# Talking-heads attention with two MLPs: v's matmuls share the slots of the scores' matmuls, first mixings are issued in twos, and GpSimd makes every third high part

## The chip, the cores and the metric

One core of a Trainium2 chip runs the whole program. The metric is device time in microseconds, the median of several runs.

## The reference

A talking-heads attention over 4 batches, 12 heads, 448 tokens and head size 64, and behind it two MLPs. Heads are mixed before and after the softmax:

```python
scores = scale * np.matmul(q, k.transpose(0, 1, 3, 2))
scores = np.einsum('bhij,hg->bgij', scores, w_pre)      # first mixing
scores = scores - np.max(scores, axis=-1, keepdims=True)
attn = np.exp(scores)
attn = attn / (np.sum(attn, axis=-1, keepdims=True) + 1e-09)
attn = np.einsum('bhij,hg->bgij', attn, w_post)         # second mixing
return np.matmul(attn, v).astype(np.float32)
```

The result, as 1792 tokens of width 768, goes through `((x @ w1) * (x @ w2)) @ w3 @ w_out` and then `relu(x @ w_in) ** 2 @ w_out`. Precision near float32 is kept by splitting a number into a high part in a short format and a low part that holds the rest; a product is then three matmuls (high times high, high times low, low times high).

## The kernel before, in words

**Blocks.** A batch's 448 rows are cut into four groups of 110, 110, 110 and 118 rows ("supers", `SUP`), 16 in all; a group is cut into blocks of 10 rows (and one of 8). There are 180 blocks (`BLK`). A block holds 10 rows of all 12 heads, 120 rows for the partitions, so that one matmul with a 120 by 120 matrix mixes the heads.

**The work of one block.** `regroup` (L259) copies the block's scores from the tile `S`, where a row is a partition, into `Bt`, by a DMA of SP's queue. `premix` (L266) is the first mixing, one float32 matmul into a bank of the PSUM ring `ps_p` (three banks). `negmax` (L278) reduces it to the maximum on VectorE; `expo` (L287) takes the exponential on ScalarE with a running sum. `norm` (L301) makes the inverse sums for two blocks at once on VectorE. `split_h` (L317) makes the high part `EH` of exponential times inverse, on VectorE; `split_l` (L325) scales the exponential in place on GpSimd (L328) and subtracts the high part from it, which gives `EL` (L331). `postmix` (L334) is the second mixing, 12 matmuls of float16 into `ps_o` (two banks). `at_h` (L352, ScalarE) and `at_l` (L361, VectorE) bring the result to SBUF as high and low part.

**The work of a group.** `qk` (L215) makes the scores of two heads, six matmuls into the one tile of `ps_s` (two banks), and `evict_s` (L238) copies them to `S` on ScalarE. `av` (L435) multiplies with v: for each pair of heads 24 matmuls in two parts of 12, collected over three pairs in the one bank of `ps_a`; `put_xh` and `put_xl` (L462, L476) read that bank and `store_x` (L484) sends it to memory. `split_q`, `split_ql`, `split_k` and `split_kl` (L197 to L213, L177 to L188) make high parts on VectorE and low parts on GpSimd. `sum_v`, `scale_v`, `split_v` and `split_vl` (L378 to L433) find v's scale and split v; two steps of `scale_v` use TensorE and a bank of `ps_p`.

**The order.** It is written by hand: a loop over slots `u` (L893 to L939) issues, in each slot, `at_h(u-5)`, `premix(u+1)`, `negmax(u)`, `expo(u)`, in even slots `norm(u-2)`, then `split_h(u-2)`, `split_l(u-2)`, `postmix(u-4)`, `at_l(u-5)`, and `regroup(u+4)` last. Work of a group is entered by `at(slot, kind, ...)` into a table of events (L504 to L556); `do(kind)` issues the events of the slot at five places: LOAD ahead of everything, FIRST in front of the exponential, MID and LOW behind `at_l`, END behind those. `qk` and `av` are END events. Every engine works through its own instructions in this order and waits where an operand is not there. From slot 168 on, weights of the MLP are loaded beside the attention, and from slot 170 on decoded; the MLPs follow.

The loop's slots of v's matmuls are offsets from five slots behind the start of the next group:

```python
AV_AT = (0, 1, 1, 2, 3, 3, 5, 6, 6, 7, 8, 8)
slot = first[s + 1] + LAG + 1 + AV_AT[2 * p + part]
at(slot, END, av, s, p, part)
```

Of the kernel before, what the change touches and what calls it, by code (L numbers as in the profile page):

```python
# [24 lines left out]
LEAD = 4  # L25
# [10 lines left out]
def talking_heads_attention_moe_moe2(  # L36
# [222 lines left out]
    def regroup(u):  # L259
        s, m, n = BLK[u]  # L260
        t = bp.tile([NBK, S], F32, tag="Bt", name="Bt", bufs=LEAD + 1)
# [16 lines left out]
    def negmax(u):  # L278

        n, j = BLK[u][2] * H, u % 2  # L280
        if j == 0:
            nsum[u] = nsum[u + 1] = bp.tile([NBK, 4, 2], F32, tag="st", name="st", bufs=3)
# [18 lines left out]
    def norm(u):  # L301

        t = nsum[u]
        rows = [BLK[x][2] * H for x in (u, u + 1)]
        for a in [slice(0, 2)] if rows[0] == rows[1] else [slice(0, 1), slice(1, 2)]:
            n = rows[a.start]
            nc.vector.tensor_scalar(  # L307
                t[:n, 2, a], t[:n, 1, a], 1e-9, 2.0 ** -11, op0=ALU.add, op1=ALU.mult
            )
        for a in [slice(0, 2)] if rows[0] == rows[1] else [slice(0, 1), slice(1, 2)]:  # L310
            n = rows[a.start]
            nc.vector.reciprocal(t[:n, 3, a], t[:n, 2, a])

    def inverse(u):
        return nsum[u][: BLK[u][2] * H, 3, u % 2 : u % 2 + 1]

    def split_h(u):  # L317
        n = BLK[u][2] * H
        hh = bp.tile([NBK, S], F16, tag="EH", name="EH", bufs=4)
        nc.vector.tensor_scalar(  # L320
            hh[:n].rearrange("p (a b) -> p a b", a=EG), Ex[u][:n], inverse(u), None, op0=ALU.mult
        )
        EH[u] = hh

    def split_l(u):  # L325
        n = BLK[u][2] * H
        e = Ex.pop(u)[:n]
        nc.gpsimd.tensor_scalar(e, e, inverse(u), 1.0, op0=ALU.mult, op1=ALU.mult)  # L328
        ll = bp.tile([NBK, S], F16, tag="EL", name="EL", bufs=4)
        a, b = (x[:n].rearrange("p (a b) -> p a b", a=EG) for x in (ll, EH[u]))  # L330
        nc.gpsimd.tensor_tensor(a, e, b, op=ALU.subtract)  # L331
# [60 lines left out]
    def scale_v(b, i):  # L392
# [5 lines left out]
        elif i == 1:  # L398
            vps[b] = pt = psum(ps_p, "p")
# [4 lines left out]
        elif i == 3:  # L404
            vps[b] = pt = psum(ps_p, "p")
# [124 lines left out]
    for b in range(B):  # L530
        f = first[4 * b]
        for hg in range(2):
            at(f - 4 + hg, LOAD, load_v, b, hg)
            for i in range(3):
                at(f + 3 * hg + i + 1, MID, sum_v, b, hg, i)
                at(f + 3 * hg + i + 11, MID, split_v, b, hg, i)
                at(f + 3 * hg + i + 12, LOW, split_vl, b, hg, i)
        for i, kind in enumerate((MID, END, MID, END, MID)):
            at(f + 6 + i, kind, scale_v, b, i)
    AV_AT = (0, 1, 1, 2, 3, 3, 5, 6, 6, 7, 8, 8)  # L540
    for s in range(NSUP - 1):
        for p in range(NDC):
            for part in range(2):
                slot = first[s + 1] + LAG + 1 + AV_AT[2 * p + part]
# [343 lines left out]
    premix(0)  # L888
    mlp_start = first[NSUP - 1]
# [3 lines left out]
    for u in range(NB + LAG + 2):  # L893
# [22 lines left out]
        if u + 1 < NB:  # L916
            premix(u + 1)
# [421 lines left out]
```

## Time and profile before

| | us |
|---|---|
| median of 3 runs | 1352.63 |
| lowest and highest run | 1351.04, 1352.71 |
| the profiled execution | 1354.19 |
| its span, first to last instruction | 1352.5 |
| TensorE busy in the span | 1289.3 (95%) |
| VectorE busy | 1035.0 (77%) |
| ScalarE busy | 712.8 (53%) |
| GpSimd busy | 442.9 (33%) |
| attention: start of the first and last first mixing | 22.3, 468.9 |

The profile is of one execution. Engines are PE (TensorE; PEld is its weight load), DVE (VectorE), ACT (ScalarE), POOL (GpSimd) and SP (a DMA queue). A name such as `EH<-E,st` stands for the tiles written and read, `o` for the bank of the second mixing, `p` for that of the first, `s` for the scores' and `a` for v's. A busy engine is not an engine that sets the time: the chain of waits goes back from the last instruction to what released it, step by step, and shows what does. The shares above are of the whole span; the attention, about a third of it, is read by its own stretches.

### The profile page before, as it was taken

Reading aid. Unit: us, or ns where it says so; the run is one execution under the profiler, and the core shown is the slowest. Engines: PE = TensorE matmul, PEld = TensorE weight load, DVE = VectorE, ACT = ScalarE, POOL = GpSimd, SP = SyncE. Lnnn points to the kernel's source line nnn. Section 1 sums busy time; section 2 is a strip of 40 time slices with the busy share of each in tenths; the row PEclk is TensorE's granted clock in tenths of the full one; section 3 lists DMA queues with packets and bytes.
Section 4 is the critical chain, followed back from the end, with each engine's and each line's share of the span. In section 5 each row is a group of like instructions: output and inputs, shape, how many; then the busy total and the mean of one; then the engine's idle time right before and its main releaser. Section 6 shows DMA issues by size and latency. Waiting matters only on the chain.

```text
span 1352.5 us, 26245 instructions
## 1 busy us (share of the span) xinstructions
PE 1289.3 (95%) x10170; PEld 790.7 (58%) x10170; DVE 1035.0 (77%) x2101; ACT 712.8 (53%) x1365; POOL 442.9 (33%) x511
## 2 busy tenths in 40 slices
PE   5999999999999789999998879999999999999998
PEld 2566666666666554555557855555555555555555
DVE  5999999899899857678836555544667797797866
ACT  3876877876776534444424444435774534535430
POOL 3889789779877621000001200000000000000000
PEclk7999999999999789999999989999999999999999
DMA  5356455544644914344503313400532214223104
GB/s 175 94 140 178 112 143 151 137 121 129 157 112 109 275 53 100 97 110 113 120 17 125 110 47 77 77 6 4 112 71 43 75 48 98 74 36 84 26 13 163
DMA packets 76096, 132.94 MB, mean 98 GB/s; under 512 B 30116, under 2 KB 59940, under 8 KB 75972
## 3 DMA queue, kind: packets, MB, share of 16 engines
q1 hardware_dynamic: 69556, 121.87, 33.7%
q0 software_dynamic: 2992, 5.42, 3.1%
q10 hardware_dynamic: 3424, 3.98, 1.1%
q8 instruction: 80, 1.31, 0.5%
q14 instruction: 44, 0.36, 0.1%
HBM read 80.78 MB, written 11.92 MB: 69 GB/s over the span
## 4 chain that ended last, share of the span: by engine, by line
PE 70%; DVE 19%; DMA 4%; ACT 4%; issue 3%; POOL 1%; SPq 0%; ACTq 0%; POOLq 0%; DVEq 0%
PE mm L982 38%; PE mm L1216 16%; PE p L269 5%; PE o L343 4%; DVE EH L320 3%; DVE ATl L365 3%; DVE st L283 3%; DMA Bt<-S 3%; PE s L229 2%; PE a L452 2%; DVE st L307 1%; DVE Vl L431 1%; PE mm L1088 1%; DVE zt L632 1%; DVE xa L635 1%
## 5 line engine op out<-in xcount | busy, mean ns | idle before, releaser
L982 PE MATMUL mm<-x,w 128*128 128x448 f16 x2304 | 438.9, 353 | 3.3 <-DVE w L717 1.7
L982 PEld LDWEIGHTS <-w 128*128 128x128 f16 x2304 | 225.5, 98 | 215.0 <-issue 2.7
L1216 PE MATMUL mm<-w,g 128*128 128x384 f16 x1344 | 219.7, 326 | 0.0
L269 PE MATMUL p<-Bt,wpre_k 120*120 120x448 f32 x360 | 184.1, 594 | 17.7 <-DMA Bt<-S 16.1
L331 POOL TENSOR_TENSOR EL<-E,EH 120x448 f16<-120x448 f32 x180 | 188.5, 1047 | 15.0
L343 PEld LDWEIGHTS <-EH 120*112 120x112 f16 (+1 forms) x1440 | 133.2, 131 | 90.0 <-issue 89.6
L1216 PEld LDWEIGHTS <-g 128*128 128x128 f16 x1344 | 131.5, 98 | 87.4 <-issue 0.2
L328 POOL TENSOR_SCALAR E<-E,st 120x448 f32<-120x448 f32 x180 | 134.5, 747 | 80.7 <-DVE EH L320 45.6
L291 ACT ACTIVATE E<-p,st 120x448 f32<-120x448 f32 x180 | 115.3, 640 | 57.5 <-DVE st L283 51.6
L343 PE MATMUL o<-wph,EH 120*112 120x120 f16 x720 | 125.7, 218 | 8.6 <-DVE ATl L365 8.4
L359 ACT CAST ATh<-o 112x480 f16<-112x480 f32 x180 | 101.0, 561 | 57.0 <-PE o L343 56.0
L343 PE MATMUL o<-wph,EL 120*112 120x120 f16 x720 | 125.6, 218 | 0.8 <-POOL EL L331 0.8
L343 PE MATMUL o<-wpl,EH 120*112 120x120 f16 x720 | 125.6, 218 | 0.0
L283 DVE TENSOR_REDUCE st<-p 120x1 f32<-120x448 f32 x180 | 110.8, 615 | 17.0 <-PE p L269 16.7
L320 DVE TENSOR_SCALAR EH<-E,st 120x448 f16<-120x448 f32 x180 | 121.3, 674 | 3.1
L1225 DVE SCALAR_TENSOR_TENSOR acc<-mm,sv,acc 128x384 f32<-128x384 f32 x196 | 112.3, 612 | 14.2 <-PE mm L1216 13.5
L653 POOL DMA_DIRECT2D across<-tot x23 | 12.8, 555 | 326.8 <-ACT xa L639 326.8
L639 ACT ACTIVATE xa<-xa 128x768 f32<-128x768 f32 (+1 forms) x72 | 57.2, 795 | 117.3 <-DVE xa L635 107.5
L365 DVE TENSOR_TENSOR ATl<-o,ATh 112x480 f16<-112x480 f32 x180 | 116.3, 646 | 2.7 <-ACT ATh L359 2.3
L982 PE MATMUL mm<-h,M 128*128 128x448 f16 x576 | 110.6, 355 | 1.7 <-ACT M L1010 1.7
L240 ACT COPY S<-s 110x896 f32<-110x896 f32 (+1 forms) x92 | 83.7, 910 | 22.3 <-PE s L229 21.9
L343 PEld LDWEIGHTS <-EL 120*112 120x112 f16 x720 | 94.7, 132 | 0.9 <-POOL EL L331 0.9
(176 smaller groups left out, 1956.5 us busy)
## 6 DMA issues: line engine op xcount, KB each, us to landing
Bt<-S SPq DMA_DIRECT2D x176, 210.0 KB
raw<-in_moe_w_out_dram SPq DMA_DIRECT2D x24, 768.0 KB
raw<-in_moe_w_in_dram SPq DMA_DIRECT2D x16, 768.0 KB
raw<-in_moe_w_dram SPq DMA_DIRECT2D x14, 768.0 KB
raw<-in_moe_w_dram SPq DMA_DIRECT2D x16, 512.0 KB
kraw<-in_k_dram SPq DMA_DIRECT2D x12, 448.0 KB
vraw<-in_v_dram SPq DMA_DIRECT2D x8, 672.0 KB
out_dram<-acc SPq DMA_DIRECT2D x28, 192.0 KB
```

Of the source, the lines that this page charges most:

```text
L269: nc.tensor.matmul(pt[: n * H, :S], wpre_k.rearrange("p t g -> p (t g)")[: n * H, : n * H], Bt.pop(u)[: n * H], start=True, stop=True,)
L283: nc.vector.tensor_reduce(nsum[u][:n, 0, j : j + 1], Pp[u][:n, :S], axis=AX.X, op=ALU.max, negate=True)
L291: nc.scalar.activation(e[:n], Pp.pop(u)[:n, :S].rearrange("p (a b) -> p a b", a=EG), AF.Exp, bias=t[:n, 0, j : j + 1], scale=1.0, accum_ou ...
L320: nc.vector.tensor_scalar(hh[:n].rearrange("p (a b) -> p a b", a=EG), Ex[u][:n], inverse(u), None, op0=ALU.mult)
L328: nc.gpsimd.tensor_scalar(e, e, inverse(u), 1.0, op0=ALU.mult, op1=ALU.mult)
L331: nc.gpsimd.tensor_tensor(a, e, b, op=ALU.subtract)
L343: nc.tensor.matmul(pt[:CP, c * n : (c + 1) * n], a[:n, c * CP : (c + 1) * CP], w[:n, :n], start=(i == 0), stop=(i == 2),)
L359: nc.scalar.copy(ATs[s][0][:, :, :, m * NR : m * NR + nr], src)
L365: nc.vector.tensor_tensor(ATs[s][1][:, :, :, a], src, ATs[s][0][:, :, :, a], op=ALU.subtract)
L982: nc.tensor.matmul(pt[:, :S], w[a][:, cs], x[z][:, sl], start=(c == 0 and i == 0), stop=(c == len(parts) - 1 and i == 2),)
L1216: nc.tensor.matmul(pt[:, :OH], gs[j][a][:, ts_], ws[j][0][:, w, os_], start=(n == 0), stop=(n == 5),)
L1225: nc.vector.scalar_tensor_tensor(d, pt[:, :OH], sv[:, v : v + 1], d, op0=ALU.mult, op1=ALU.add)
```

## The change

Five edits, all in the attention:

1. `regroup` is issued five slots ahead (LEAD 4 to 5), with as many tiles `Bt` as before (five).
2. `norm` writes the sum plus 1e-9, times a constant, three times into `t[:, 2:5, :]`, reading the two columns with a stride of nought; the inverses move to row 5. Only pairs of blocks of unequal size are done one by one.
3. The high part of every block with `u % 3 == 2` is made on GpSimd in `split_l`. The scaled exponential goes to a tile of its own, `F` (one buffer), and not over `E`.
4. Two steps of `scale_v` use the scores' tile `ps_s`, not a bank of `ps_p`; the steps and `split_v`, `split_vl` move one to two slots back.
5. Both parts of `av` for a pair of heads go to one slot, that of one of the next group's `qk` where six of them fall into its span, and else to fixed offsets. `premix` is issued for two blocks at once in odd slots and not at all in even ones.

```diff
-LEAD = 4
+LEAD = 5
...
-        t = bp.tile([NBK, S], F32, tag="Bt", name="Bt", bufs=LEAD + 1)
+        t = bp.tile([NBK, S], F32, tag="Bt", name="Bt", bufs=LEAD)
...
-            nsum[u] = nsum[u + 1] = bp.tile([NBK, 4, 2], F32, tag="st", name="st", bufs=3)
+            nsum[u] = nsum[u + 1] = bp.tile([NBK, 6, 2], F32, tag="st", name="st", bufs=3)
...
+        if rows[0] == rows[1]:
+            n = rows[0]
+            nc.vector.tensor_scalar(
+                t[:n, 2:5, :],
+                t[:n, 1, :].unsqueeze(1).to_broadcast([n, 3, 2]),
+                1e-9, 2.0 ** -11, op0=ALU.add, op1=ALU.mult,
+            )
+        else:
+            for a in (0, 1):
+                n = rows[a]
+                nc.vector.tensor_scalar(
+                    t[:n, 2, a : a + 1], t[:n, 1, a : a + 1], 1e-9, 2.0 ** -11,
+                    op0=ALU.add, op1=ALU.mult,
+                )
         for a in [slice(0, 2)] if rows[0] == rows[1] else [slice(0, 1), slice(1, 2)]:
             n = rows[a.start]
-            nc.vector.tensor_scalar(
-                t[:n, 2, a], t[:n, 1, a], 1e-9, 2.0 ** -11, op0=ALU.add, op1=ALU.mult
-            )
...
-            nc.vector.reciprocal(t[:n, 3, a], t[:n, 2, a])
+            nc.vector.reciprocal(t[:n, 5, a], t[:n, 2, a])
...
+    def high_on_pool(u):
+        return u % 3 == 2
 
     def split_h(u):
         n = BLK[u][2] * H
-        hh = bp.tile([NBK, S], F16, tag="EH", name="EH", bufs=4)
-        nc.vector.tensor_scalar(
-            hh[:n].rearrange("p (a b) -> p a b", a=EG), Ex[u][:n], inverse(u), None, op0=ALU.mult
-        )
-        EH[u] = hh
+        EH[u] = bp.tile([NBK, S], F16, tag="EH", name="EH", bufs=4)
+        if not high_on_pool(u):
+            nc.vector.tensor_scalar(
+                EH[u][:n].rearrange("p (a b) -> p a b", a=EG), Ex[u][:n], inverse(u), None,
+                op0=ALU.mult,
+            )
 
     def split_l(u):
         n = BLK[u][2] * H
         e = Ex.pop(u)[:n]
-        nc.gpsimd.tensor_scalar(e, e, inverse(u), 1.0, op0=ALU.mult, op1=ALU.mult)
+        f = bp.tile([NBK, EG, EW], F32, tag="F", name="F", bufs=1)[:n, :, : S // EG]
         ll = bp.tile([NBK, S], F16, tag="EL", name="EL", bufs=4)
         a, b = (x[:n].rearrange("p (a b) -> p a b", a=EG) for x in (ll, EH[u]))
-        nc.gpsimd.tensor_tensor(a, e, b, op=ALU.subtract)
+        nc.gpsimd.tensor_scalar(f, e, inverse(u), 1.0, op0=ALU.mult, op1=ALU.mult)
+        if high_on_pool(u):
+            nc.gpsimd.tensor_scalar(b, e, inverse(u), 1.0, op0=ALU.mult, op1=ALU.mult)
+        nc.gpsimd.tensor_tensor(a, f, b, op=ALU.subtract)
         EL[u] = ll
...
-            vps[b] = pt = psum(ps_p, "p")
+            vps[b] = pt = ps_s.tile([P, 2, 512], F32, tag="s", name="s")[:, 0]
...
-                at(f + 3 * hg + i + 11, MID, split_v, b, hg, i)
-                at(f + 3 * hg + i + 12, LOW, split_vl, b, hg, i)
-        for i, kind in enumerate((MID, END, MID, END, MID)):
-            at(f + 6 + i, kind, scale_v, b, i)
-    AV_AT = (0, 1, 1, 2, 3, 3, 5, 6, 6, 7, 8, 8)
+                at(f + 3 * hg + i + 13, MID, split_v, b, hg, i)
+                at(f + 3 * hg + i + 14, LOW, split_vl, b, hg, i)
+        for i, (slot, kind) in enumerate(((7, MID), (9, END), (10, MID), (11, END), (12, MID))):
+            at(f + slot, kind, scale_v, b, i)
+    qk_at = sorted(x for x in events if any(e[2] is qk for e in events[x]))
     for s in range(NSUP - 1):
         for p in range(NDC):
+            lo = first[s + 1] + LAG + 1
+            at_qk = [x for x in qk_at if lo <= x < lo + SUP[s + 1][3]]
+            slot = at_qk[p] if len(at_qk) == NDC else lo + (0, 1, 3, 4, 6, 7)[p]
             for part in range(2):
-                slot = first[s + 1] + LAG + 1 + AV_AT[2 * p + part]
                 at(slot, END, av, s, p, part)
...
     premix(0)
+    premix(1)
...
-        if u + 1 < NB:
-            premix(u + 1)
+        if u % 2:
+            for x in (u + 1, u + 2):
+                if x < NB:
+                    premix(x)
```

The change of the bank in `scale_v` is made in both of its steps that use TensorE.

## Rows read from the trace of the kernel before

**Rows 1.** Stretch, its us, busy PE, PEld, DVE, ACT, POOL, clock, DMA, GB/s.

```profile
100.00:400.00 300.00, 292.68 (x3642) 200.81 (x3638) 280.44 (x586) 228.28 (x502) 253.73 (x281) 0.99 0.53 139
```

**Rows 2.** The chain of waits, 100 to 400 us, shares by line.

```profile
by line: PE p L269 20.9%; PE o L343 14.9%; PE s L229 10.3%; PE a L452 9.3%; DVE ATl L365 8.0%; DVE st L283 7.6%; DVE EH L320 7.3%; DMA Bt<-S 4.7%; issue 4.1%; DVE Vl L431 3.2%; DVE st L307 2.9%; DVE xt L480 1.4%; DVE st L312 1.3%; DVE kh L1
```

**Rows 3.** The chain of waits in a clean stretch: start us, us, what.

```profile
247.94 0.70 PE a L452 x24
248.65 0.94 PE p L269 x2
249.59 0.63 PE o L343 x12
250.22 0.80 PE p L269 x2
...
256.22 0.43 PE a L452 x12
...
258.23 0.74 PE a L452 x24
```

**Rows 4.** Timeline, TensorE, end of the attention: start us, us, instruction.

```profile
471.18 0.19 PE L452 MATMUL s<-ATh,Vl 112*64 112x40 f16 x2
471.30 0.26 PE L343 MATMUL o<-wph,EH 120*112 120x120 f16 x1
471.39 0.22 PE L343 MATMUL o<-wpl,EH 120*112 120x120 f16 x1
```

**Rows 5.** Timeline, ScalarE, the clean stretch.

```profile
253.79 0.20 ACT L291 ACTIVATION_READ_ACCUMULATOR E<-p,st 120x1 f32 x1
```

**Rows 6.** Instructions by line, 100 to 400 us: busy us, mean ns, idle before.

```profile
L331 POOL TENSOR_TENSOR EL<-E,EH 120x448 f16<-120x448 f32 (+1 forms) x122 | 127.7, 1047 | 10.2
...
L328 POOL TENSOR_SCALAR E<-E,st 120x448 f32<-120x448 f32 (+1 forms) x121 | 88.5, 731 | 36.0 <-DVE EH L320 15.0 <-PE o L343 4.7 <-ACT E L291 3.9
...
L307 DVE TENSOR_SCALAR st<-st 120x2 f32<-120x2 f32 (+2 forms) x64 | 23.5, 370 | 0.0
L188 POOL TENSOR_TENSOR kl<-kraw,kh 128x448 fp32r<-128x448 f32 x16 | 21.2, 1326 | 0.0
L213 POOL TENSOR_TENSOR ql<-qraw,qh 128x330 fp32r<-128x330 f32 (+1 forms) x22 | 20.3, 922 | 0.0
...
L182 DVE CAST kh<-kraw 128x448 fp32r<-128x448 f32 x15 | 9.0, 603 | 0.0
```

**Rows 7.** One line each: its instructions, ns min/median/max, first and last start.

```profile
L307 DVE TENSOR_SCALAR st<-st x94: 132/266/956, 28.5 to 472.6; 120x2 f32<-120x2 f32 x86, 96x1 f32<-96x1 f32 x4, 120x1 f32<-120x1 f32 x4
...
L312 DVE RECIPROCAL st<-st x94: 140/166/167, 28.7 to 472.8; 120x2 f32<-120x2 f32 x86, 96x1 f32<-96x1 f32 x4, 120x1 f32<-120x1 f32 x4
...
L320 DVE TENSOR_SCALAR EH<-E,st x180: 657/674/681, 28.9 to 474.2; 120x448 f16<-120x448 f32 x176, 96x448 f16<-96x448 f32 x4
...
L182 DVE CAST kh<-kraw x24: 377/384/1330, 5.0 to 335.8; 128x448 fp32r<-128x448 f32 x24
...
L328 POOL TENSOR_SCALAR E<-E,st x180: 631/642/2369, 29.8 to 475.6; 120x448 f32<-120x448 f32 x176, 96x448 f32<-96x448 f32 x4
...
L331 POOL TENSOR_TENSOR EL<-E,EH x180: 1002/1012/1586, 30.5 to 478.0; 120x448 f16<-120x448 f32 x176, 96x448 f16<-96x448 f32 x4
```

**Rows 8.** Who waited for whom, 49 to 432 us: us, times, longest.

```profile
PE o L343 <- DVE ATl L365: 6.6, 14, 0.9
...
PE p L269 <- DMA Bt<-S: 2.8, 2, 2.0
```

**Rows 9.** Who waited for whom, SP's queue, whole span.

```profile
SPq L174 <- POOL kl L188: 16.4, 3, 5.6
```

**Rows 10.** Timeline, GpSimd, two blocks in steady work.

```profile
299.42 0.64 POOL L328 TENSOR_SCALAR E<-E,st 120x448 f32<-120x448 f32 x1
300.15 1.01 POOL L331 TENSOR_TENSOR EL<-E,EH 120x448 f16<-120x448 f32 x1
301.14 0.64 POOL L328 TENSOR_SCALAR E<-E,st 120x448 f32<-120x448 f32 x1
```

More of the change, by code (lines that the diff above doesn't have):

```diff
@@ L304, in norm @@
         rows = [BLK[x][2] * H for x in (u, u + 1)]
+        if rows[0] == rows[1]:
[12 more added lines that the diff above has]
+                )
         for a in [slice(0, 2)] if rows[0] == rows[1] else [slice(0, 1), slice(1, 2)]:
             n = rows[a.start]
-            nc.vector.tensor_scalar(
-                t[:n, 2, a], t[:n, 1, a], 1e-9, 2.0 ** -11, op0=ALU.add, op1=ALU.mult
-            )
-        for a in [slice(0, 2)] if rows[0] == rows[1] else [slice(0, 1), slice(1, 2)]:
-            n = rows[a.start]
-            nc.vector.reciprocal(t[:n, 3, a], t[:n, 2, a])
+            nc.vector.reciprocal(t[:n, 5, a], t[:n, 2, a])
     def inverse(u):
-        return nsum[u][: BLK[u][2] * H, 3, u % 2 : u % 2 + 1]
+        return nsum[u][: BLK[u][2] * H, 5, u % 2 : u % 2 + 1]
+    def high_on_pool(u):
+        return u % 3 == 2
     def split_h(u):
         n = BLK[u][2] * H
-        hh = bp.tile([NBK, S], F16, tag="EH", name="EH", bufs=4)
-        nc.vector.tensor_scalar(
-            hh[:n].rearrange("p (a b) -> p a b", a=EG), Ex[u][:n], inverse(u), None, op0=ALU.mult
-        )
-        EH[u] = hh
+        EH[u] = bp.tile([NBK, S], F16, tag="EH", name="EH", bufs=4)
[4 more added lines that the diff above has]
+            )
     def split_l(u):
@@ L404, in scale_v @@
         elif i == 3:
-            vps[b] = pt = psum(ps_p, "p")
+            vps[b] = pt = ps_s.tile([P, 2, 512], F32, tag="s", name="s")[:, 0]
             nc.tensor.matmul(pt[:, :1], ones[:1], m[:1, 7:8], start=True, stop=True)
```

## The prediction

> **What bounds the kernel now.** I read the busy time by stretch first, then the chain of waits, then single instructions. Between 100 and 400 us, the steady part of the attention, TensorE is busy 292.68 of 300 us, VectorE 280.44, GpSimd 253.73 [rows 1]: two engines near their limit and a third not far behind. The chain of waits over the same stretch agrees: 55% of it is TensorE's four lines (L269, L343, L229, L452), about a third is VectorE (L365, L283, L320, L307 and smaller ones) [rows 2]. The stretch holds 121 blocks (121 scales of L328 [rows 6]), so a block costs 300 / 121 = 2.48 us. What the change can win has to be told for each engine apart: what TensorE needs for a block, what VectorE's lateness adds, and what GpSimd would allow.
>
> Of the 180 blocks I count the middle 156. The first 12 fill the pipeline and have scores in nearly each slot; beside the last 12 the MLP's weights are loaded and decoded. I expect no gain from either.
>
> **TensorE: v's matmuls beside the scores'.** The chain of a clean stretch gives prices [rows 3]. A first mixing takes 0.80 us behind a postmix and 0.94 behind anything else; twelve matmuls of v take 0.43 us behind scores, twenty-four 0.70, and twenty-four in a slot of their own 0.74 plus the 0.14 by which the next mixing is dearer, 0.88. Twelve alone I put at 0.43 + 0.14 = 0.57. I laid the two schedules out slot by slot from the code. Before, 25 slots hold scores with 24, 35 scores with 12, 37 hold 24 alone, 25 hold 12 alone: 17.5 + 15.1 + 32.6 + 14.3 = 79.5 us. After, 79 hold scores with 24 (55.3 us) and some 14 hold v's alone (11.8): 67.1 us. That is 12.4 us less, 11 of it in the middle.
>
> **TensorE: mixings in pairs.** The second of a pair follows a mixing, not v or scores, which would take 0.14 us from some 99 mixings, 13.9 us. But in the other slot a postmix now stands behind v's matmuls. At the end of the attention there are such cases: the postmix starts 0.12 us after the last v matmul has started and its next step comes after 0.09 us [rows 4], where its steps are else 0.05 apart (0.63 us for twelve [rows 3]). That is 0.07 + 0.04 = 0.11 us, nearly what the mixing paid: the switch is moved and not saved. Bounds 0 and -13.9 us (-12 in the middle); I take 0, by that row.
>
> What this edit needs is a bank of PSUM in time. The first mixings have three, so the second of a pair needs the exponential of the block two before it, where it was three before. From a block's mixing to the second one of the next pair there are 2 x 2.4 + 0.8 = 5.6 us. The mixing that ends at 251.02 in the chain [rows 3] is read out by its exponential until 253.99 [rows 5], 3.0 us after its end, 3.8 after its start: covered, in a clean stretch. Each microsecond by which VectorE lags comes off these 1.8.
>
> **Regrouping five ahead.** The ring of Bt stays at five tiles, so the DMA of a tile waits for the mixing five blocks back as it did; its place in SP's queue moves one slot, ahead of the next slot's loads and stores. For odd blocks the pair takes back what that gives. Cost 0, hidden by the slots between issue and use, unless SP is held in front of it. It was: the load of k waits for GpSimd's low part of k, 16.4 us in 3 waits [rows 9], and TensorE waited up to 2.0 us for Bt [rows 8]. A later GpSimd makes that longer; it is counted there.
>
> **VectorE.** It loses a third of the high parts, 40 of 121 at 0.67 us [rows 7], and the long form of the norm: L307 takes 370 ns in the mean [rows 6] and 132 at least [rows 7], (370 - 150) x 64 = 14 us. Together 41 of 280 us, so it goes from 93% to about 80% and is no longer late as a rule. TensorE's wait that names it is the postmix's for L365, 6.6 us in 14 [rows 8]; I take 6 us away (bounds 0 and, with what reaches TensorE by way of ScalarE, 12).
>
> Whether L307 gets short is not sure. This operation on two columns takes up to 956 ns, the reciprocal of the same shape never over 167 [rows 7]; and GpSimd's scale takes 731 ns in the mean [rows 6] against a median of 642 [rows 7]. So the two engines hold each other up there. The new form reads three rows (the same two columns again and again) and writes six columns in one run. The nearest row is the high part L320: seven rows read, one run of 448 written, 657 to 681 ns and never longer, where the cast of k, 448 columns in one run, takes 377 at best and 1330 at worst [rows 7]. So an odd number of rows written to one run is slower and is not held up, and I take the short form. The Trainium skill ("Advanced Engine Details and Errata", VectorE Performance Modes, Mode Summary) says that two-port instructions of VectorE and GpSimd's block each other, and that the two-port mode is taken where the outer dimensions of source and destination are both even, or both odd and equal. By that rule, with three rows on both sides, the new form would still be held up and the 14 us would be nought; by the row of L320 they are won.
>
> **GpSimd.** Scale and subtract take 1.72 us per block (299.42 to 301.14 [rows 10]). F is one tile, so the next scale has to wait for the last subtract. What such a wait costs shows between scale and subtract: 0.09 us from end to start, where from subtract to scale it is -0.02 [rows 10]. Bounds 0 and 0.11 us a block; I take 0.11, since it is the same kind of wait. The high part is a scale with one input: 0.64 us like L328, or at most the subtract's 1.01, which also writes two-byte values [rows 7]; I take 0.64, the same operation. Then GpSimd needs for the 121 blocks: 121 x 1.83 = 221.4; 40 x 0.64 = 25.6; low parts of q 20.3 and of k 21.2 [rows 6]; and, of the (731 - 642) x 121 + (1047 - 1012) x 122 = 15 us by which VectorE holds it up now, the share of the cast of k, (603 - 384) x 15 = 3.3 against L307's 14, so 2.9. Sum 291 of 300 us. **GpSimd becomes the tightest engine**, and the most that the middle can win is 9 x 156 / 121 = 11 us, where TensorE alone would win 17.
>
> It is not spread evenly. Three times, for 12 slots, k of the next batch is split. There GpSimd needs 12 x 2.23 + 6 x 1.33 = 34.7 us, TensorE some 28.5. Of these 6 us about 3 are covered: a block is split two slots before its postmix, 4.8 us, and takes 1.83. TensorE waits about 3 us each time, 9 in all, where I estimate 4 now (2.8 of them for Bt [rows 8]). That gives 5 us back (bounds 0 and 13).
>
> **v's scale in the scores' bank.** Scores in the same slot as the scale's read now wait for VectorE, which has some three operations like L320 (0.67 us [rows 7]) ahead of it, against 0.63 for the postmix [rows 3]. In even slots, where no mixing stands in front, I estimate 0.8 us, in four cases: +3 us (bounds 0 and 8).
>
> **Sum.** -11 (v beside scores) + 0 (pairs) - 6 (VectorE's lateness) + 5 (GpSimd while k is split) + 3 (v's scale) = -9 us, within the 11 that GpSimd allows. The profiled execution took 1354.19 us (a span of 1352.5 and 1.7 around it), 1.6 above the median of 1352.63. The differences apply to either: 1354.2 - 9 = 1345.2 for such an execution, and 1352.6 - 9 = 1343.6 us for the median, which I forecast. The MLP behind the attention is not touched and moves up by what that saves.
>
> **Rivals.** *GpSimd is no limit and the pairs pay.* If the subtract does not hold the next scale, GpSimd needs 13 us less in the stretch, and with the pairs' 12 TensorE sets the time: 1343.6 - 12 = 1331.6. For it: the 0.14 us of [rows 3]. Against it: the postmix of [rows 4]. *The norm does what it did* (three rows still held up): GpSimd keeps the other 12 us of its hold-ups and needs 303 of 300: 3 x 156 / 121 = 4 us slower, 1356.6. This is the outcome by the rule of the Trainium skill's Mode Summary, told above. Against it stands L320. *GpSimd gets slower than the kernel is now.* The place is the high part in split_l, the price its duration. 9 us over 40 such operations are left, so from 0.64 + 0.22 = 0.86 us on it decides against the change; at the subtract's 1.01 GpSimd needs 306, which is 6 x 156 / 121 = 8 us slower, 1360.6. For it: the subtract writes two-byte values too. Against it: one input, like the scale.
>
> **Chances.** Forecast 0.56, GpSimd no limit 0.18, norm as it was 0.10, GpSimd slower 0.12, anything else 0.04. The range runs from 1329, which takes in most of the second case, to 1357, which takes in the third; the fourth and the tail of the second are left out. About 0.2%, 2.7 us, is what a measurement of this kernel can tell from no change. The forecast's own bounds reach it at one end only, so faster 0.54 + 0.18 + 0.03 = 0.75, within 0.2% 0.10, slower 0.15.
>
> **What would show it.** L307 at some 160 ns in each instance and GpSimd's scale at 642 ns in the mean show the norm right. GpSimd over 95% busy between 100 and 400 us, with scales that start 0.09 us after a subtract ends, shows its limit; VectorE should fall to about 80%. In the chain a mixing behind a mixing should cost 0.80 us, and a postmix behind v more than one behind a mixing. The prediction is wrong if GpSimd is often idle while a block takes under 2.35 us (then the pairs pay), or if mixings wait for exponentials or for Bt in every other slot (then the pairs starve).

## The result and the profile after

The changed kernel takes **1364.51 us** (median of four runs; the three compared lie between 1362.08 and 1364.87), the kernel before 1351.84 us beside it. The ratio is 1.0088 with a 95% interval of 1.0072 to 1.0103: slower by about 12 us, where 9 us faster was forecast. The profiled execution took 1364.16 us (span 1362.4). The fourth run, of 2596.25 us, and one of 2525.12 us among those of a version below took about twice as long and are left out of the ratios.

The loss lies in the attention. TensorE's second mixing of block 179, the last, starts at 478.1 us in the trace of before and at 488.5 us after; the MLP behind it takes as long as before. In the stretch from 100 to 400 us, read as [rows 1]:

```profile
100.00:400.00 300.00, 277.18 (x3491) 190.54 (x3489) 230.33 (x520) 212.53 (x479) 271.02 (x311) 0.99 0.52 135
```

TensorE was busy 292.68 us there before and VectorE 280.44 [rows 1]; now it is 277 and 230. GpSimd went up, from 253.73 to 271.02. No engine is as busy as TensorE was, and yet the stretch holds 116 blocks where it held 121 (second mixings begun in it). So the time went into waits: TensorE's matmuls stand still 22.8 us of the 300, 7.3 before. The chain of waits (shares by line, and three of its longest pieces: start us, us, what), against [rows 2]:

```profile
by line: PE p L269 20.7%; PE o L359 16.7%; DMA Bt<-S 16.4%; PE s L229 10.7%; PE a L468 8.6%; POOL EL L347 6.1%; issue 4.7%; POOL F L344 3.6%; DVE st L283 2.1%; DVE Vl L447 1.6%; DVE ATl L381 1.2%; ACT ATh L375 1.0%; POOL EH L346 1.0%; ACT S
...
127.65 10.25 DMA Bt<-S
243.29 10.36 DMA Bt<-S
...
357.75 11.62 DMA Bt<-S
```

The transfers of `Bt` were 4.7% of the chain before [rows 2] and are 16.4% now, the longest in pieces of 10 to 12 us. Such a piece is the whole transfer from its issue on; TensorE's own wait at its end is shorter. Who waited for whom, 49 to 432 us (us, times, longest), against [rows 8]:

```profile
PEld p L269 <- ACT E L291: 13.5, 28, 1.6
...
PEld L359 <- POOL EL L347: 12.8, 18, 1.2
...
PE o L359 <- POOL EL L347: 10.1, 13, 1.0
PE p L269 <- DMA Bt<-S: 9.1, 6, 3.0
...
PE p L269 <- ACT E L291: 2.8, 4, 0.9
...
PE o L359 <- DVE ATl L381: 1.9, 3, 0.8
```

The rows of PEld and of PE are not to be added: a weight load waits for the same thing as the matmul behind it (all 13 waits of matmuls for `EL` end with one of the 18 of weight loads, and all 4 for exponentials with one of the 28). What TensorE's matmuls lost stands in the rows of PE. Second mixings wait 10.1 us for GpSimd's `EL` (none before), first mixings 9.1 us for `Bt` (2.8 before) and only 2.8 for exponentials (0.8 before). The wait for VectorE's `ATl`, 6.6 us before, is down to 1.9: VectorE was relieved as planned.

The long waits for `Bt` cost more than their length. TensorE's granted clock is at the lower of its two levels, 1.2 GHz and not 2.4 (0.50 in the profile), from 335.0 to 338.4 us and from 369.1 to 372.5, just where waits of 2.1 and 3.0 us for `Bt` end, at 335.0 and 369.5. Before, it is so once between 100 and 400 us, from 327.0 to 330.4, behind a wait of 2.0 us for `Bt` that ends at 325.7.

**Where along the attention.** For each trace I took the start of the second mixing of a block (the first of its twelve matmuls in TensorE's timeline) at a few blocks, and subtracted. The stretches repeat for each of the three later batches: blocks 25 to 37, 70 to 82 and 115 to 127, where k is split ("k"); blocks 37 to 48, 82 to 93 and 127 to 138, where the first group of a new batch begins and its v is loaded ("v"); and the rest ("plain"). Differences in us; each cell names the three stretches of a kind. A trace is one execution and can lie up to some 4 us off its kernel's median, so a difference counts that comes back in the three stretches.

| traces | up to block 25 | k | v | plain | block 160 to 179 |
|---|---|---|---|---|---|
| changed − before | −0.9 | +3.8, +4.2, +2.2 | +0.2, +1.8, +2.7 | −0.9, −0.9, −0.1 | −1.7 |

So the change does gain in plain stretches, a little, and loses some 10 us where k is split and 5 us where v is loaded. The experiments take these apart. Two theories were named before the first run: **G**, that GpSimd cannot keep up where k is split, and **P**, that pairs starve, for an exponential or for `Bt`.

### The profile page after: what moved, and what is told of

It is laid out like the page before. It is cut to its first block, busy times and chain, and to the rows that moved or that the text cites. A ratio compares the mean times of both kernels' runs of the same rounds, so it can differ in the third digit from the quotient of the medians.

```text
span 1362.4 us, 26289 instructions
## 1 busy us (share of the span) xinstructions
PE 1285.4 (94%) x10170; PEld 789.1 (58%) x10170; DVE 980.1 (72%) x2041; ACT 707.4 (52%) x1365; POOL 481.3 (35%) x571
## 4 chain that ended last, share of the span: by engine, by line
PE 74%; DVE 9%; DMA 5%; ACT 5%; POOL 3%; issue 3%; SPq 0%; ACTq 0%; POOLq 0%; DVEq 0%
PE mm L1003 39%; PE mm L1237 16%; PE p L269 7%; PE o L359 5%; DMA Bt<-S 4%; PE s L229 3%; PE a L468 3%; POOL EL L347 2%; DVE st L283 1%; POOL F L344 1%; DVE zt L650 1%; DVE ATl L381 1%; DVE Vl L447 1%; DVE xa L653 1%; ACT xa L657 1%
## 5 line engine op out<-in xcount | busy, mean ns | idle before, releaser
L347 POOL TENSOR_TENSOR EL<-F,EH 120x448 f16<-120x448 f32 x180 | 194.5, 1080 | 20.1 <-DVE EH L333 4.2
L269 PE MATMUL p<-Bt,wpre_k 120*120 120x448 f32 x360 | 167.2, 582 | 21.4 <-DMA Bt<-S 16.6
L359 PEld LDWEIGHTS <-EH 120*112 120x112 f16 (+1 forms) x1440 | 127.5, 132 | 51.6 <-issue 45.1
L344 POOL TENSOR_SCALAR F<-E,st 120x448 f32<-120x448 f32 x180 | 127.0, 706 | 45.3 <-DVE st L321 32.7
L359 PE MATMUL o<-wph,EL 120*112 120x120 f16 x720 | 126.1, 220 | 10.1 <-POOL EL L347 10.1
L359 PE MATMUL o<-wph,EH 120*112 120x120 f16 x720 | 128.5, 222 | 6.3 <-DVE ATl L381 6.1
L283 DVE TENSOR_REDUCE st<-p 120x1 f32<-120x448 f32 x180 | 110.8, 616 | 17.6 <-PE p L269 15.4
L269 PEld LDWEIGHTS p<-Bt,wpre_k 120*120 120x120 f32 x360 | 59.3, 188 | 70.2 <-issue 39.8
```

The costliest lines, as they stand in the source:

```text
L269: nc.tensor.matmul(pt[: n * H, :S], wpre_k.rearrange("p t g -> p (t g)")[: n * H, : n * H], Bt.pop(u)[: n * H], start=True, stop=True,)
L283: nc.vector.tensor_reduce(nsum[u][:n, 0, j : j + 1], Pp[u][:n, :S], axis=AX.X, op=ALU.max, negate=True)
L344: nc.gpsimd.tensor_scalar(f, e, inverse(u), 1.0, op0=ALU.mult, op1=ALU.mult)
L347: nc.gpsimd.tensor_tensor(a, f, b, op=ALU.subtract)
L359: nc.tensor.matmul(pt[:CP, c * n : (c + 1) * n], a[:n, c * CP : (c + 1) * CP], w[:n, :n], start=(i == 0), stop=(i == 2),)
```

## The experiments

Times are medians; a ratio is to the kernel before on the same chip, with its 95% interval. 0.1% is 1.35 us.

### High parts on VectorE, pairs kept

```diff
     def high_on_pool(u):
-        return u % 3 == 2
+        return False
```

> The changed kernel with all high parts on VectorE again (60 operations of 0.64 us less on GpSimd, 60 of 0.67 us more on VectorE); everything else as changed. Theory G (GpSimd cannot keep up in the three stretches where k is split; postmixes wait for EL there, some 15 us in all): 12 to 16 us under the changed kernel, 1347 to 1352 us, and the waits of postmixes for EL nearly gone. Theory P (the second mixing of a pair waits for an exponential or for Bt): within 4 us of the changed kernel, 1359 to 1366, and the mixings' waits stay.

1359.82 us, ratio 1.006 (1.0043 to 1.0078). Who waited for whom, 49 to 432 us:

```profile
PEld p L269 <- ACT E L291: 19.5, 35, 2.1
...
PE p L269 <- ACT E L291: 3.0, 5, 0.9
...
PEld L359 <- POOL EL L347: 2.1, 6, 0.7
...
PE o L359 <- POOL EL L347: 1.0, 2, 0.6
```

The matmuls' wait for `EL` fell from 10.1 to 1.0 us, but the time by only 0.3%. The wait for exponentials rose to 19.5 us at the weight loads and is 3.0 at the matmuls, where it was 2.8. Block by block the edit does what G said and takes it back elsewhere: against the changed kernel the three stretches of k are 4.2, 4.4 and 4.3 us shorter, and the plain ones, where VectorE makes every high part again, 1.8, 1.3 and 1.8 us longer. G is a part and not the whole.

### Pairs undone

```diff
-        if u % 2:
-            for x in (u + 1, u + 2):
-                if x < NB:
-                    premix(x)
+        if u + 1 < NB:
+            premix(u + 1)
```

> The changed kernel with one first mixing per slot again, as before the change; everything else as changed. G: within 3 us of the changed kernel, 1360 to 1366 us, since GpSimd's work is the same. P: 8 us or more under it, 1355 or less, and the mixings' waits for exponentials (now 16 us between 49 and 445 us) mostly gone.

1354.05 us, ratio 1.0012 (0.9999 to 1.0026): 0.76% below the changed kernel, 10 us. With one mixing in a slot the change is about even with the kernel before, and from 49 to 432 us its first mixings wait 0.8 us for `Bt` and not at all for exponentials.

### The norm on two columns, and no F

```diff
-                t[:n, 2:5, :],
-                t[:n, 1, :].unsqueeze(1).to_broadcast([n, 3, 2]),
+                t[:n, 2, :],
+                t[:n, 1, :],
```

> The changed kernel with the norm's first operation on two columns again, written once; everything else as changed. G: the hold-ups come back to GpSimd and the stretches get longer: 5 to 12 us over the changed kernel, 1368 to 1376 us, L307 at some 370 ns. P: 0 to 4 us over it.

1362.48 us, ratio 1.0079 (1.0058 to 1.01). No difference to the changed kernel, where G had it 5 to 12 us slower: its VectorE is busy 230 us of 300, and here 244. The other edit lets GpSimd scale in place again, behind the high part:

```diff
-        f = bp.tile([NBK, EG, EW], F32, tag="F", name="F", bufs=1)[:n, :, : S // EG]
...
-        nc.gpsimd.tensor_scalar(f, e, inverse(u), 1.0, op0=ALU.mult, op1=ALU.mult)
         if high_on_pool(u):
             nc.gpsimd.tensor_scalar(b, e, inverse(u), 1.0, op0=ALU.mult, op1=ALU.mult)
-        nc.gpsimd.tensor_tensor(a, f, b, op=ALU.subtract)
+        nc.gpsimd.tensor_scalar(e, e, inverse(u), 1.0, op0=ALU.mult, op1=ALU.mult)
+        nc.gpsimd.tensor_tensor(a, e, b, op=ALU.subtract)
```

> The changed kernel without the tile F: GpSimd makes the high part first where it has to, then scales the exponential in place. The scale does not wait for the last subtract (0.11 us a block less on GpSimd), but where VectorE makes the high part it waits for that again. G: 3 to 8 us under the changed kernel, 1355 to 1361, with scales that start without a gap behind subtracts in the stretches where k is split. P: within 3 us of it.

1360.73 us, ratio 1.007 (1.0046 to 1.0095): 2 us lower by the ratios, and the intervals overlap.

### v's slots alone, and pairs alone, on the kernel before

The first of these takes only the new slots of v's matmuls over (the part of the diff behind `qk_at`), the second only the pairs with what they need (`LEAD = 5`, five buffers for `Bt`, v's scale in the scores' bank).

> The kernel before with v's matmuls in the slots of the scores' matmuls and nothing else of the change. If the entry into v's matmuls and back is saved as the prediction has it: 5 to 11 us below before, 1342 to 1348 us. Rival: VectorE and the Bt transfers set the pace as before and what TensorE saves comes back as their waits: 1350 to 1354 us.

1358.19 us, ratio 1.003 (1.0016 to 1.0043): slower than either form of the expectation. From 100 to 400 us, in an execution of 1353.93 us, the fastest of its eleven:

```profile
100.00:400.00 300.00, 286.29 (x3624) 196.79 (x3624) 278.06 (x584) 227.39 (x502) 254.09 (x280) 1.00 0.51 139
```

TensorE has 6.4 us less to do than before (286.29 against 292.68 [rows 1]) at nearly the same pace, 3624 matmuls for 3642. VectorE is at 278.06, as it was. The saving is there and turns into waiting: from 49 to 432 us the matmuls wait 9.7 us for `ATl` and 6.1 for `Bt`, 6.6 and 2.8 before [rows 8].

> The kernel before with pairs (and what they need: regrouping five ahead with five buffers, v's scale in the scores' bank), v's matmuls in their old slots, norm, high parts and GpSimd as before. Theory P: 1358 to 1366 us, mixings waiting for exponentials and for Bt. Rival, theory G alone with pairs free, as the prediction had it: 1350 to 1354 us.

1363.87 us, ratio 1.007 (1.0049 to 1.0092). Pairs cost 0.7% by themselves, with GpSimd as it was. From 49 to 432 us the matmuls of the first mixings wait 8.4 us for `Bt`, 2.8 before, and 3.0 us for exponentials (16.3 at the weight loads).

### Pairs undone and high parts on VectorE

Both edits above together.

> One first mixing per slot as before, and every high part on VectorE; v's matmuls stay in the slots of the scores', and so do the norm, F and the early regrouping. Theory P with G (pairs cost some 10 us, GpSimd's high parts some 5 us, v's slots gain on TensorE): both costs are gone and the gain is left, 1345 to 1350 us, and postmixes no longer wait for EL. Rival: v's slots are worth nothing at the end, or only in company with the pairs: 1352 to 1356 us, about the kernel before.

1349.99 us, ratio 0.9961 (0.9947 to 0.9974): faster than before. Against the run with pairs (1.006) pairs cost 1.0% here. So in three settings they cost 0.7, 0.76 and 1.0%, 9 to 13 us.

### What v's slots and the norm are worth in that version

> The fastest version so far with v's matmuls back in their old slots (norm, F, early regrouping and v's scale stay). If v's slots gain on TensorE what the prediction said, once VectorE is relieved: 1355 to 1361 us, 5 to 11 above. Rival (v's slots gain nothing; the gain of that version is VectorE's and the regrouping's): 1346 to 1352 us.

With the old slots of v's matmuls: 1351.08 us, ratio 0.9982 (0.9968 to 0.9996). v's slots are worth 0.2% here, 3 us, with intervals that just overlap; the forecast had 11.

> The fastest version so far (unpaired, high parts on VectorE, 1349.99 us) with the norm on two columns again. Theory V (in that version the six columns are what makes it faster, since VectorE is still 90 percent busy there): the norm costs 0.2 us per pair again and the time goes up to 1353 to 1358 us. Rival (VectorE's 0.1 us per block stays beside TensorE, as in the paired kernel, where the norm's form made no difference): 1349 to 1351 us.

With the norm on two columns: 1355.25 us, ratio 1.0024 (1.0012 to 1.0035). The six columns are worth 0.6%, 8 us, where VectorE is busy 272.5 us of 300, and nothing where it is busy 230.

### Why pairs cost: the ring, the place, the transfers

```diff
-        t = bp.tile([NBK, S], F32, tag="Bt", name="Bt", bufs=LEAD)
+        t = bp.tile([NBK, S], F32, tag="Bt", name="Bt", bufs=LEAD + 1)
```

> The changed kernel with six buffers for Bt where it has five, and F left out to make the room (the run without F alone gave 1360.73 us). Pairs kept. Theory P, first form (the second mixing of a pair is starved by Bt, whose ring of five leaves odd blocks a slot less): 1351 to 1355 us, and TensorE's mixings wait for Bt as little as before (2.8 us from 49 to 432 us). Theory P, second form (it is starved by the exponential two blocks back, through the three banks): within 3 us of 1360.7, the mixings still wait for E 12 us or more.

1359.08 us, ratio 1.0035 (1.0022 to 1.0049), against 1.007 (1.0046 to 1.0095) without F alone: 2 us better by the medians, 5 by the ratios, with intervals that just overlap. That is within what the second form of the theory allows. The mixings waited for `Bt` as long as ever, which the first form did not expect:

```profile
PE p L269 <- DMA Bt<-S: 10.6, 7, 2.8
```

SP's queue waits less for the mixings to give a buffer free (41.7 us from 49 to 432 us, 83.5 in the changed kernel), so transfers are issued earlier, and some still land late. The ring is at most a part of it. Next comes the place of the pair, with high parts on VectorE: the loop over `u + 1, u + 2` moved from ahead of `negmax(u)` to behind `postmix(u - LAG)`.

> Pairs, high parts on VectorE (as in the first run, 1359.8 us), and the pair issued behind the slot's second mixing instead of ahead of it. Theory P, second form (the pair comes to TensorE before the exponentials have freed its banks): the exponentials get 0.7 us more, the mixings wait for E under 10 us from 49 to 432 us (20.3 us from 100 to 400 us in the first run) and the time falls to 1350 to 1356 us. Rival: a pair starves the other engines by its burst, whatever stands ahead of it (the next two first mixings are a longer way off for VectorE and ScalarE): 1358 to 1362 us.

1362.35 us, ratio 1.0068 (1.0045 to 1.0091), no better than 1.006. Waits, 49 to 432 us:

```profile
PE o L359 <- DVE ATl L381: 17.0, 22, 1.9
...
PEld p L269 <- ACT E L291: 5.4, 16, 2.5
```

The wait for exponentials fell from 19.5 to 5.4 us at the weight loads and from 3.0 us to none at the matmuls, and the matmuls' wait for `ATl` rose from 7.4 to 17.0 us. The wait was moved by the place of the pair and not cured, so the exponentials alone are not the cause; whether the burst of two mixings costs in itself, this run does not tell.

The table by stretch told more. Pairs against no pairs, at the same setting otherwise:

| traces | up to block 25 | k | v | plain | block 160 to 179 |
|---|---|---|---|---|---|
| pairs alone − before | −0.2 | +0.6, +1.1, −1.3 | +3.5, +2.2, +3.5 | +1.2, +1.6, +1.7 | +3.3 |
| changed − pairs undone | +4.0 | −1.2, −0.2, −0.4 | 0.0, +2.2, +2.8 | +1.1, +1.3, +1.0 | +1.5 |
| with − without pairs, high parts on VectorE | −0.8 | +1.2, +0.4, +1.3 | +1.4, +2.3, −0.1 | −0.3, −0.1, −0.3 | +0.9 |

Of the steps that come back in several stretches, the largest stand where v is loaded. SP's queue in the changed kernel there (start us, us, instruction, count), with the wait of the mixings from 355 to 375 us and what the queue moved in that stretch (packets, MB, share of the engines' time; KB of one transfer):

```profile
355.33 0.48 SPq L387 DMA_DIRECT2D vraw<-in_v_dram  x1
355.92 1.19 SPq L263 DMA_DIRECT2D Bt<-S  x1
357.16 0.49 SPq L387 DMA_DIRECT2D vraw<-in_v_dram  x1
357.75 1.16 SPq L263 DMA_DIRECT2D Bt<-S  x1
359.00 0.84 SPq L194 DMA_DIRECT2D qraw<-in_q_dram  x1
359.94 0.81 SPq L263 DMA_DIRECT2D Bt<-S  x1
```

```profile
PE p L269 <- DMA Bt<-S: 3.0, 1, 3.0
```

```profile
q1 hardware_dynamic: 2259, 3.63, 75.2%
...
Bt<-S SPq DMA_DIRECT2D x8, 210.0 KB
vraw<-in_v_dram SPq DMA_DIRECT2D x2, 672.0 KB
qraw<-in_q_dram SPq DMA_DIRECT2D x1, 330.0 KB
```

Two loads of 672 KB and one of 330 KB are issued between 355.3 and 359.8 us. The queue moves 3.63 MB in 20 us, so these 1.67 MB are an estimated 9 us of its work, and the `Bt` issued at 357.75 us between them, that of block 137, lands 11.62 us later, as the chain above has it. The six waits for `Bt` from 49 to 432 us are those of blocks 35, 47, 91, 93, 125 and 137 (1.7, 1.2, 0.5, 0.6, 2.1 and 3.0 us), all odd: the second of a pair, which TensorE now wants one slot earlier than before, while its buffer still comes free with the mixing five blocks back. Four of them stand where v is loaded, two where k is. This can be tested without touching the pairs, by issuing v's two loads seven and five slots earlier (the expectation says four):

```diff
-            at(f - 4 + hg, LOAD, load_v, b, hg)
+            at(f - (11, 8)[hg] if b else f - 4 + hg, LOAD, load_v, b, hg)
```

> Pairs, high parts on VectorE (the first run, 1359.8 us), and v's two loads of the second to fourth batch issued seven and four slots earlier, away from the border of two superblocks. Theory B (pairs cost where Bt lands late behind v's loads: block by block this version lost 1.4 us from slot 41 to 52 and 2.3 us from slot 86 to 97 against the unpaired one, and nothing in the plain stretches): 1353 to 1357 us, the waits of the mixings of blocks 46, 47, 90 to 92, 136 and 137 gone. Rival (the burst of a pair itself): 1358 to 1362 us.

1355.18 us, ratio 1.0017 (1.0007 to 1.0028), from 1.006: as theory B said.

> The changed kernel with v's loads earlier in the same way and nothing else. Theory B: 1357 to 1361 us, 3 to 7 below the changed kernel; what is left above the kernel before is GpSimd's while k is split. Rival (the burst): 1362 to 1366 us.

1357.52 us, ratio 1.0042 (1.0027 to 1.0057), from 1.0088, again by theory B. The mixings' wait for `Bt`, 49 to 432 us, was 9.1 us:

```profile
PE p L269 <- DMA Bt<-S: 2.7, 2, 1.3
```

> Control: unpaired, high parts on VectorE (1349.99 us) with v's loads earlier. Theory B: no change beyond 2 us, 1348 to 1352 us, since without pairs hardly a mixing waits there. Rival (late Bt costs with and without pairs): 1343 to 1347 us.

1348.83 us, ratio 0.9977 (0.9967 to 0.9987), from 0.9961: the control gains nothing, and the rival, which had it gain too, falls.

| traces | up to block 25 | k | v | plain | block 160 to 179 |
|---|---|---|---|---|---|
| changed, v's loads earlier − changed | −1.0 | +0.7, 0.0, −0.5 | −1.5, −1.9, −4.8 | 0.0, 0.0, −0.1 | +2.0 |

Moving v's two loads takes 0.46% off the changed kernel, 6 us, and by the trace just where v was loaded. Of the 4.8 us in the last of these stretches 3.0 are the wait for `Bt`. The other 1.8 are matmul time, 26.4 us against 24.6: with the loads moved, the clock stays at its higher level there. With pairs, `Bt` lands late behind a bulk load; without them the same loads hide.

### GpSimd where k is split

Pairs undone; every third high part on GpSimd, except near the splitting of k:

```diff
-        return u % 3 == 2
+        return u % 3 == 2 and not (u >= 22 and (u - 22) % 45 < 17)
```

> Unpaired, every third high part on GpSimd except in the three stretches where k is split. Theory G (GpSimd's high parts cost only where k is split): as fast as with all high parts on VectorE or faster, 1343 to 1350 us. Rival (GpSimd's high parts cost everywhere, or save nothing once TensorE sets the pace): 1350 to 1354 us.

**1340.44 us, ratio 0.991 (0.9892 to 0.9928)**: the fastest of all, faster than both kernels. From 100 to 400 us, and its waits from 49 to 432 us:

```profile
100.00:400.00 300.00, 293.39 (x3698) 200.85 (x3699) 252.00 (x565) 230.10 (x510) 276.16 (x310) 1.00 0.52 138
```

```profile
PEld L359 <- POOL EL L347: 7.4, 26, 0.4
...
PE o L359 <- POOL EL L347: 3.0, 15, 0.3
...
PE p L269 <- DMA Bt<-S: 1.0, 2, 0.8
```

With the high parts left on GpSimd everywhere (pairs undone, above), these waits for `EL` were 13.9 us at the weight loads and 8.7 at the matmuls, and GpSimd was full where k is split (columns as in [rows 1]):

```profile
76.00:106.00 30.00, 27.19 (x321) 17.91 (x320) 21.57 (x50) 19.30 (x41) 28.39 (x31) 0.97 0.50 140
```

28.4 of 30 us; in the other two stretches (188 to 218 and 301 to 331 us) it is 28.39 and 28.40. In the fastest kernel GpSimd is as full there (28.21 us from 74 to 104 us), so what differs is how much it has to do for the same blocks. From the second mixing of block 23 to that of block 35, and 45 and 90 blocks on, GpSimd works 30.7 to 32.6 us in 32.3 to 34.2 with every third high part, 28.3 to 29.5 us in 29.9 to 31.1 with those outside k, and 26.4 to 26.5 us in 28.0 with none (pairs undone, high parts on VectorE). It is 95% busy each time, and the stretch is as long as its work makes it.

| traces | up to block 25 | k | v | plain | block 160 to 179 |
|---|---|---|---|---|---|
| pairs undone, high parts everywhere − outside k | +0.4 | +3.5, +3.0, +2.9 | −0.4, −0.3, +0.5 | 0.0, +0.6, 0.0 | −0.8 |
| pairs undone, high parts all on VectorE − every third on GpSimd | +5.3 | −6.6, −5.0, −6.0 | +0.9, −0.6, −0.5 | +3.1, +2.8, +3.1 | +3.1 |
| pairs undone, high parts outside k − before | −5.3 | +1.5, +1.4, −0.3 | +0.6, −0.1, −0.7 | −1.9, −2.8, −1.1 | −2.4 |

Without pairs G is shown: 9.4 us in the trace, 1.0% in the ratios, and all of it where k is split. With no high part on GpSimd at all these stretches are 17.6 us shorter, but the plain ones 9.0 longer.

> The fastest version (unpaired, high parts on GpSimd outside the stretches of k, 1340.44 us) with v's loads earlier. Theory B (without pairs Bt is in time, its waits there were 1.0 us in all): 1338 to 1342 us.

1342.17 us, ratio 0.9925 (0.9913 to 0.9938): nothing to gain there without pairs.

### Both cures with the pairs kept

> The changed kernel with both cures and its pairs: v's loads earlier, and no high part on GpSimd where k is split. Theories B and G together, if their costs add (some 6 and some 10 us): 1345 to 1350 us, below the kernel before and some 5 above the unpaired kernel with both (1342.17 us). Rival (with GpSimd relieved the pairs' rest is gone too, it was the wait for EL): 1340 to 1344 us. Rival (the costs are the same microseconds): 1352 to 1357 us.

1353.68 us, ratio 1.0011 (1.0 to 1.0022), which is what the third of these expectations said. The two cures do not add: high parts outside k gave 0.3% here and 1.0% without pairs. Pairs still cost 0.86% against the run without them, 11.6 us. By the table of stretches 7.9 us of that lie where k is split (+4.9, +1.0, +2.0), where loads of k and now also v's are issued. In the first of these the mixings of blocks 35 and 39 wait 1.2 and 2.9 us for `Bt`, and behind the second wait, which ends at 115.7 us, the clock is at its lower level from 116.1 to 119.5 us. Long pieces of the chain there (start us, us, what):

```profile
98.85 4.66 DMA Bt<-S
107.11 8.47 DMA Bt<-S
224.54 9.79 DMA Bt<-S
```

> That kernel with the third load of k issued two slots later, so that SP's queue is not held by GpSimd (21.9 us in three waits in the changed kernel) with Bt behind it. Theory K (the pairs' rest is Bt late behind this hold): 3 to 5 us below the run ahead of it. Rival (the rest is the pair itself): within 1.5 us of it.

1352.93 us, ratio 0.9998 (0.9985 to 1.0011), with a wide spread (1345.93 to 1354.4): within 1.5 us of the run ahead, as the rival said. The hold itself was halved and not removed, from 19.4 to 9.9 us (49 to 432 us). In the profiled execution, 1349.29 us and so one of its fastest, the first stretch of k got 3.1 us shorter, without the wait of 2.9 us and the lower clock behind it, and the other two by 0.0 and 0.3; the median does not tell it from the run ahead.

## Why the prediction was wrong

With the edits taken in one by one, the ratios go down by 0.2% for the norm, `F`, the early regrouping and v's scale, by 0.2% for v's slots, and up by 0.5% for the high parts on GpSimd and by 0.8% for the pairs: 0.9% in all, 12 us (another order would share it out otherwise). Where the forecast had −11 us and 0, for v's slots and for the pairs, this has −3 and +10.

**What failed** is the step "Regrouping five ahead", with "Cost 0, hidden by the slots between issue and use, unless SP is held in front of it", and with it the 0 for the pairs. Pairs cost 9 to 13 us. I had seen that "for odd blocks the pair takes back what that gives", and asked only whether SP's queue is held. Where v is loaded it was not held: the transfer itself takes 10 to 12 us when v's loads are in front of it. Some 6 of the pairs' 10 us are shown to be this. The rest is not settled. In the plain stretches and at the start a further 3 and 4 us of the changed kernel vanish with the pairs; small waits of several kinds are seen there (from block 48 to 70 the matmuls wait 0.7 us for exponentials and 0.5 for the copy of scores to `S`, and without pairs not at all), and none could be shown to be the cause. TensorE's own side of the pairs came out near the 0 of the forecast: the matmuls of these blocks take 51.8 us with pairs and 52.0 without. The banks were not much of it either. With three of them a mixing needs the exponential of the block three back in both kernels, and not "two before it" as I wrote; the 5.6 us between the two were right, and matmuls waited 2.8 us for exponentials from 49 to 432 us, where I had them covered. A fourth bank for the first mixings was not tried; it would have had to be taken from another ring.

**v beside the scores, −11.** TensorE did get its saving (6.4 us in 300, alone), but the time did not: +0.3% alone on the kernel before, −0.2% with VectorE relieved. I took a saving on one of two engines that are both near their limit (97.6 and 93.5% of the stretch [rows 1]) for a saving on the path.

**GpSimd while k is split, +5 (bounds 0 and 13).** Mis-sized: against the kernel before, the three stretches are 12.0 us longer with pairs undone, 9.4 of which go with the high parts near k. I had worked out 34.7 us for GpSimd in twelve slots and then called half of the excess covered by the two slots of lead. With pairs undone the three stretches take 35.1, 33.4 and 34.5 us, against 30.1, 29.1 and 31.9 before: they came out at GpSimd's own sum, and the lead covered next to nothing of it. Over all of 100 to 400 us GpSimd is busy 90% in the changed kernel, and not over 95 as forecast: its limit shows where k is split.

**GpSimd's hold-ups.** I put 12 of 15 us of them down to L307 and took them away. They stayed: from 100 to 400 us the scale takes 702 ns in the mean, where I had said 642, and the subtract went from 1047 [rows 6] to 1076 (columns as there, with the shapes). The long ones stand beside other operations (last section).

```profile
L347 POOL TENSOR_TENSOR EL<-F,EH 120x448 f16<-120x448 f32 x115 | 123.7, 1076 | 12.9 <-DVE EH L333 3.4 <-POOL F L344 0.2
L344 POOL TENSOR_SCALAR F<-E,st 120x448 f32<-120x448 f32 x114 | 80.0, 702 | 14.8 <-DVE st L321 7.0 <-ACT junk L402 0.3 <-POOL EL L347 0.2
```

The norm's long form and the high part, against [rows 7]:

```profile
L307 DVE TENSOR_SCALAR st<-st x86: 135/149/161, 27.8 to 476.4; 120x6 f32<-120x6 f32 x86
...
L346 POOL TENSOR_SCALAR EH<-E,st x60: 632/641/1271, 33.9 to 484.7; 120x448 f16<-120x448 f32 x56, 96x448 f16<-96x448 f32 x4
```

L307 is never held up, 135 to 161 ns, as L320's row had it; the Trainium skill's rule in "Advanced Engine Details and Errata", VectorE Performance Modes, Mode Summary, under which three rows on both sides would share a port with GpSimd, does not describe this form. The high part costs 0.64 us in the median, as forecast, so the rival in which it is dearer fell. F's wait is as forecast too, 0.10 us from the end of a subtract to the next scale, where it was −0.02 [rows 10]:

```profile
250.07 0.65 POOL L344 TENSOR_SCALAR F<-E,st 120x448 f32<-120x448 f32 x1
250.80 1.01 POOL L347 TENSOR_TENSOR EL<-F,EH 120x448 f16<-120x448 f32 x1
251.91 0.64 POOL L344 TENSOR_SCALAR F<-E,st 120x448 f32<-120x448 f32 x1
```

**VectorE, −6.** Right in sign. With pairs undone, the high parts taken from VectorE are worth 9.0 us in the plain stretches (table above). Without pairs and with GpSimd kept free of high parts where k is split, the change gains 5.8 us in the plain stretches and 12 us in all; and the norm's form, to which I gave no place of its own on the path, is worth 8 us where VectorE is tight.

**v's scale, +3.** The scores' matmuls waited 2.3 us for it in the changed kernel (4 waits over the span), within the bounds.

Of the rivals, "GpSimd no limit and the pairs pay" is refuted: with GpSimd relieved the pairs still lose. "The norm does what it did" came out in its effect, since GpSimd kept its hold-ups, but by another cause. What came nearest is the last way of being wrong that the prediction named, mixings that wait for exponentials or for `Bt` in every other slot: they did wait for `Bt`, but at six places and not in every other slot. I gave it no price, and no chance beyond the 0.04 for anything else.

## What to carry to other kernels

A reordering that asks for an operand one slot earlier has to be checked at the slots where the same queue also carries bulk loads, by the landing time of a transfer there and not in a clean stretch. Work moved to an engine with slack on average should be kept out of the stretches in which that engine already has extra work: the same edit, with those stretches left out, went from even to 0.9% faster without pairs. And where two engines are both near their limit, a saving on one alone may be worth nothing: here v's slots saved TensorE 6.4 us in 300 and the kernel lost 0.3%. Last, a row of weight loads and a row of matmuls that wait for the same thing are one wait, not two.

## What the runs showed of the hardware

GpSimd's operations often take longer beside VectorE's casts of q and k. In the changed kernel, VectorE's and GpSimd's timelines around 240 us:

```profile
240.01 0.66 DVE L381 TENSOR_TENSOR ATl<-o,ATh 112x480 f16<-112x480 f32 x1 [0.30 <-ACT ATh L375]
240.59 0.32 DVE L205 CAST qh<-qraw 128x330 fp32r<-128x330 f32 x1
240.83 0.62 DVE L283 TENSOR_REDUCE st<-p 120x1 f32<-120x448 f32 x1
```

```profile
240.13 1.29 POOL L344 TENSOR_SCALAR F<-E,st 120x448 f32<-120x448 f32 x1
241.40 0.64 POOL L346 TENSOR_SCALAR EH<-E,st 120x448 f16<-120x448 f32 x1
```

A cast of 0.32 us falls into a scale, and the scale takes 1.29 us in place of 0.64: 0.65 more. Most scales that hold a whole cast of q are 0.5 us longer. I went through the trace of before from 100 to 400 us and noted which instructions of VectorE overlap each scale and each subtract, and which of these take over 0.06 us more than the median. All 19 scales beside a cast of q (L205) are long, with 9.6 of the 10.9 us by which scales are too long in all; and all 13 long subtracts ran beside L431, v's low part. It is not the casts alone: none of the 8 subtracts beside a cast of q or k is long there, and in the changed kernel 14 of 15 are. Of the 25 long scales only 7 overlap L307, of 23 that do, and these runs try it too: with pairs undone and high parts on VectorE, GpSimd's scales take 691 ns in the mean with the norm on six columns and 704 with it on two, its subtracts 1072 and 1066. So the norm's form is not what lengthens them. An operation that is held up by another engine need not be the one that holds that engine up: the row of L307, 132 to 956 ns [rows 7], showed the first and I read the second into it.
